# Start-up of a two-layer kernel on one core: first two token tiles enter the V projection centred, first V weights second in the load queue, dummy matmuls in the gaps

## The chip, the cores and the metric

The kernel runs on one core of one Trainium2 chip. The metric is the time of one execution in microseconds (us); lower is better. The kernel before was given with 1294.41 us, the median of 3 runs (1294.16 to 1294.68). Kernels of one group of runs were timed on one chip, interleaved with the kernel before; different groups fell on different chips.

A time is about 2.1 us longer than the span of the same run in the profile, which counts from the first to the last instruction. Times are compared with times and spans with spans.

## The reference

The model is a pair of blocks (local dilated attention, then a token-mixing MLP), run twice. Only the first lines of the first attention matter here:

```python
def _layernorm(x, axis=-1, eps=1e-5):
    m = jnp.mean(x, axis=axis, keepdims=True)
    v = jnp.var(x, axis=axis, keepdims=True)
    return (x - m) / jnp.sqrt(v + eps)
...
    # _A_ref: qkv = layernorm(x) @ wqkv, attention in a window of 8, dilation 2, then @ wo
    x = x + _A_ref(_layernorm(x, axis=-1), A_wqkv, A_wo)      # x: [1, 2048, 1024], wqkv: [1024, 3072]
    x = x + _B_ref(_layernorm(x, axis=-1), B_w1, B_b1, B_w2, B_b2)
    ...                                                        # both once more
```

## The kernel before

In lists and views, PE is TensorE, ACT is ScalarE, DVE is VectorE, and SP (SyncE) issues the loads; PSUM is the memory that TensorE writes its results to. All that the change touches is the function `start_up`, which loads the 16 token tiles (128 tokens x 1024 each), normalises them, transposes them to `hT` and multiplies them with the V weights. The first five tiles are transposed on TensorE (`tr`) and copied out of PSUM by ScalarE (`C_`), the others by DMA (`T_`). One tile passes: statistics on VectorE (`S_` twice, `A_`), 1/std on ScalarE (`R_`, a Ln and an Exp), normalisation on VectorE (`N_`), `tr`, `C_` in two halves, eight V matmuls per 512 output columns (`V_`), evacuation of PSUM on ScalarE (`E_`). Each engine gets its list in an order written by hand:

```python
    wm = m_tile()
    for _ in range(14):                    # dummy matmuls on zeros
        chain_("PE", lambda: nc.tensor.matmul(wm[:], lhsT=warm[:, 0:P], rhs=warm[:], start=True, stop=True))
    ...
    chain_("SP", x_load, 0, halves)        # load queue: tiles x0, x1, ... and halves of the V weights w(n, half)
    chain_("SP", x_load, 1)
    chain_("SP", w_load, 0, 0)
    chain_("SP", x_load, 2)
    chain_("SP", w_load, 0, 1)
    chain_("SP", x_load, 3)
    chain_("SP", w_load, 1, 0)
    chain_("SP", w_load, 1, 1)
    ...
    pe = [(tr, 0), (V_, 0, 0, lo4), (tr, 1), (V_, 0, 0, hi4), (V_, 1, 0, lo4), (tr, 2), (V_, 1, 0, hi4),
          (V_, 2, 0, a8), (V_, 0, 1, a8), (tr, 3), (V_, 1, 1, a8), (V_, 2, 1, a8), (tr, 4)]
    pe += [(V_, k, n, a8) for k in range(3, NT) for n in range(NDC)]
    act = [(R_, 0), (C_, 0, 0), (R_, 1), (C_, 0, 1), (C_, 1, 0), (C_, 1, 1), (R_, 2), (E_, 0, 0), (C_, 2, 0), (C_, 2, 1),
           (E_, 1, 0), (R_, 3), (E_, 2, 0), ...]
    dve = [(S_, 0, 0), (S_, 0, 1), (A_, 0), (S_, 1, 0), (N_, 0, halves), (S_, 1, 1), (A_, 1), (N_, 1, whole),
           (S_, 2, 0), (S_, 2, 1), (A_, 2)]
    ...
```

`(V_, k, n, lo4)` is the first half (four matmuls) of the V projection of tile k into columns 512n to 512n+511; it needs only the weight half w(n,0). V results share two PSUM buffers, so the third one waits for the evacuation of the first.

The softmax here doesn't subtract the row's maximum and nothing guards it: scores larger than these inputs give would overflow.

Of the kernel before, what the change touches and what calls it, by code (L numbers as in the profile page):

```python
# [9 lines left out]
ACT = mybir.ActivationFunctionType  # L10
# [15 lines left out]
def kernel(  # L26
# [58 lines left out]
    def m_tile():  # L85
        return psm.tile([P, 512], FP32, name="m", tag="m")
# [16 lines left out]
    def x2(name, shape=None, dt=BF16):  # L103
        return x2p.tile(shape or [P, D], dt, name=name, tag="x2")
# [4 lines left out]
    def st(name, shape):  # L109
        return stat.tile(shape, FP32, name=name, tag=name)  # L110

    def ln_exp_table():
        return tc.keep_in_program_order(nc.scalar.preload_act_table_set("natural_log_exp_and_others"))

    ln_exp_table()
    ident = const.tile([P, P], BF16, name="ident")
    make_identity(nc, ident[:])
    eps1 = const.tile([P, 1], FP32, name="eps1")
# [9 lines left out]
    for r in range(P // KG):  # L128
        hb_ = band[r * KG:(r + 1) * KG]
        nc.gpsimd.affine_select(out=hb_, in_=hb_, compare_op=ALU.is_ge, fill=0.0, base=0,  # L130
                                pattern=[[1, GW]], channel_multiplier=-1)
        nc.gpsimd.affine_select(out=hb_, in_=hb_, compare_op=ALU.is_ge, fill=0.0, base=W - 1,
                                pattern=[[-1, GW]], channel_multiplier=1)
    b1_bf = const.tile([P, FT], BF16, name="b1_bf")
    b2_bf = const.tile([P, NI, DIL], BF16, name="b2_bf")
    b1_sb = const.tile([P, FT], FP32, name="b1_sb")
# [35 lines left out]
    def rsqrt(dst, var, mul, eps):  # L172
        ln = st("ln", [P, 1])
        nc.scalar.activation(out=ln[:], in_=var, func=ACT.Ln, bias=eps[:], scale=mul)  # L174
        return nc.scalar.activation(out=dst, in_=ln[:], func=ACT.Exp, scale=-0.5)
# [9 lines left out]
        return mv[:, 0:1], rs  # L185

    def norm_dve(dst, x, mean, rs):
        return nc.vector.tensor_scalar(out=dst, in0=x, scalar1=mean, scalar2=rs[:], op0=ALU.subtract, op1=ALU.mult)

    def norm_act(dst, x, mean, rs):  # L190
        bi = st("bi", [P, 1])
# [8 lines left out]
    def chain_(eng, f, *args):  # L200
        with tc.issue_after(last[eng].ins) if eng in last else nullcontext():
            last[eng] = f(*args)

    def start_up(v, wv):
        np_ = 5
        warm = x2("warm", [P, 512])
        nc.vector.memset(warm[:], 0.0)
        xs, tps, pss_, mvs, sts, rss = {}, {}, {}, {}, {}, {}

        def x_load(k, hs=(slice(0, D),)):  # L210
            c, i = order[k]
            if k % 2 == 0:
                x_load.t = gop.tile([P, GF, D], BF16, name="x0", tag="go")
            xs[k] = x_load.t[:, k % 2, :]
            for h in hs:
                r = nc.sync.dma_start(out=xs[k][:, h], in_=xin_v[c, i][:, h])
            return r

        def w_load(n, hf):
            return nc.sync.dma_start(out=wv[n][hf][:], in_=wq_v[:, hf * (KD // 2):(hf + 1) * (KD // 2),  # L220
                                                                2 * D + n * 512:2 * D + (n + 1) * 512])

        def S_(k, cc):
            if cc == 0:
                sts[k] = st("bn", [P, NDC, 6])
            return nc.vector.bn_stats(out=sts[k][:, cc, :], in_=xs[k][:, cc * 512:(cc + 1) * 512])

        def A_(k):
            mvs[k] = st("mv", [P, 2])
            return nc.vector.bn_aggr(out=mvs[k][:], in_=sts[k][:])  # L230

        def R_(k):
            rss[k] = st("rs", [P, 1])
            return rsqrt(rss[k][:], mvs[k][:, 1:2], 1.0, eps1)

        def N_(k, hs):
            for h in hs:
                r = norm_dve(xs[k][:, h], xs[k][:, h], mvs[k][:, 0:1], rss[k])
            return r

        def tr(k):
            tps[k] = pss.tile([P, KD, P], BF16, name="s", tag="s")
            for kt in range(KD):
                r = nc.tensor.transpose(tps[k][:, kt, :], xs[k][:, kt * P:(kt + 1) * P], ident[:])
            return r

        def C_(k, hf):
            ks = slice(hf * KD // 2, (hf + 1) * KD // 2)
            return nc.scalar.copy(out=hT[:, ks, cols(*order[k])], in_=tps[k][:, ks, :])  # L249

        def V_(k, n, kts):
            if kts[0] == 0:
                pss_[k, n] = m_tile()
            for kt in kts:
                r = nc.tensor.matmul(pss_[k, n][:], lhsT=hT[:, kt, cols(*order[k])], rhs=wv[n][kt // 4][:, kt % 4, :],  # L255
                                     start=(kt == 0), stop=(kt == KD - 1))
            return r

        def E_(k, n):
            c, i = order[k]  # L260
            return nc.scalar.copy(out=v[c][i][:, n * 512:(n + 1) * 512], in_=pss_[k, n][:])

        def T_(k):
            return nc.sync.dma_start_transpose(out=hT[:, :, cols(*order[k])], in_=xs[k])

        wm = m_tile()
        for _ in range(14):
            chain_("PE", lambda: nc.tensor.matmul(wm[:], lhsT=warm[:, 0:P], rhs=warm[:], start=True, stop=True))  # L268

        halves = (slice(0, D // 2), slice(D // 2, D))  # L270
        whole = (slice(0, D),)
        chain_("SP", x_load, 0, halves)
        chain_("SP", x_load, 1)
        chain_("SP", w_load, 0, 0)
        chain_("SP", x_load, 2)
        chain_("SP", w_load, 0, 1)
        chain_("SP", x_load, 3)
        chain_("SP", w_load, 1, 0)
        chain_("SP", w_load, 1, 1)
        for k in range(4, NT):  # L280
            chain_("SP", x_load, k)

        lo4, hi4 = range(KD // 2), range(KD // 2, KD)
        a8 = range(KD)
        pe = [(tr, 0), (V_, 0, 0, lo4), (tr, 1), (V_, 0, 0, hi4), (V_, 1, 0, lo4), (tr, 2), (V_, 1, 0, hi4),
              (V_, 2, 0, a8), (V_, 0, 1, a8), (tr, 3), (V_, 1, 1, a8), (V_, 2, 1, a8), (tr, 4)]
        pe += [(V_, k, n, a8) for k in range(3, NT) for n in range(NDC)]
        act = [(R_, 0), (C_, 0, 0), (R_, 1), (C_, 0, 1), (C_, 1, 0), (C_, 1, 1), (R_, 2), (E_, 0, 0), (C_, 2, 0), (C_, 2, 1),
               (E_, 1, 0), (R_, 3), (E_, 2, 0), (R_, 4), (E_, 0, 1), (C_, 3, 0), (C_, 3, 1), (R_, 5), (E_, 1, 1), (R_, 6),
               (E_, 2, 1), (C_, 4, 0), (C_, 4, 1)]  # L290
        es = [(E_, k, n) for k in range(3, NT) for n in range(NDC)]
        rs = [(R_, k) for k in range(7, NT)]
        for j, e in enumerate(es):
            act.append(e)
            if rs and j % 4 != 3:
                act.append(rs.pop(0))
        dve = [(S_, 0, 0), (S_, 0, 1), (A_, 0), (S_, 1, 0), (N_, 0, halves), (S_, 1, 1), (A_, 1), (N_, 1, whole),
               (S_, 2, 0), (S_, 2, 1), (A_, 2)]
        for k in range(2, NT):
            nx = k + 1 < NT  # L300
            if nx:
                dve.append((S_, k + 1, 0))
            dve.append((N_, k, whole))
            if nx:
                dve += [(S_, k + 1, 1), (A_, k + 1)]
        dve.append((zero_fill,))
        dve.append((cast_biases,))
        sp = [(T_, k) for k in range(np_, NT)] + [(load_biases,)]
        qs = {"PE": pe, "ACT": act, "DVE": dve, "SP": sp}
        need = {cast_biases: lambda: (load_biases,) in done, R_: lambda k: k in mvs, N_: lambda k, h: k in rss, tr: lambda k: (N_, k) in done, C_: lambda k, hf: k in tps,  # L310
                V_: lambda k, n, kts: ((C_, k, 1 if kts[-1] == KD - 1 else 0) in done or (T_, k) in done), E_: lambda k, n: (V_, k, n) in done,
                T_: lambda k: (N_, k) in done}
        done = set()
        while any(qs.values()):
            for eng, q in qs.items():
                while q and (q[0][0] not in need or need[q[0][0]](*q[0][1:])):
                    f, *args = q.pop(0)
                    chain_(eng, f, *args)
                    if f is V_:
                        if args[2][-1] == KD - 1:  # L320
                            done.add((f, args[0], args[1]))
                    else:
                        done.add((f, *(args if f is C_ else args[:1])))

    def load_wv():
        return [[wt_("wv", [P, KD // 2, 512]) for _ in range(2)] for _ in range(NDC)]
# [256 lines left out]
    def gemm2(c, i, w2t, g, src, dst, to_hT):  # L583
# [17 lines left out]
            nc.sync.dma_start(out=dst, in_=xo[:])  # L601
        if to_hT:
            mean, rs = stats(xo, 1.0, eps1)
            norm_dve(xs[:], xo[:], mean, rs)
            nc.sync.dma_start_transpose(out=hT[:, :, cols(c, i)], in_=xs[:])

    NU = NG * DIL
# [124 lines left out]
```

## Time and profile before

| | before |
|---|---|
| time, median of 3 | 1294.41 us |
| span of the profiled run | 1293.7 us |
| TensorE (PE) busy | 1276.5 us, 99% |
| first V matmul | 8.61 us |
| V matmuls go on after the transposes of tile 4 | 21.54 us |

From the page, span and busy time of the engines:

```profile
span 1293.7 us, 19400 instructions
...
PE 1276.5 (99%) x8286; PEld 593.7 (46%) x8442; DVE 417.3 (32%) x852; ACT 373.2 (29%) x628; POOL 2.4 (0%) x15
```

TensorE is the limit, and the change can win only time in which it waits or does dummy work before the V stream is dense. This is TensorE's timeline at the start (start us, duration us, engine, line, what x count, in brackets the idle time just before it and what ended it):

```profile
1.38 6.11 PE L268 MATMUL m<-warm 128*128 128x512 bf16 x14 [1.38 <-DVE warm L207]
7.32 0.61 PE L244 MATMUL s<-ident,x 128*128 128x128 bf16 x8
8.61 1.04 PE L255 MATMUL m<-wv,hT 128*128 128x512 bf16 x4 [0.68 <-ACT hT L249]
9.62 0.62 PE L244 MATMUL s<-ident,x 128*128 128x128 bf16 x8
10.08 1.89 PE L255 MATMUL m<-wv,hT 128*128 128x512 bf16 x8
12.42 0.62 PE L244 MATMUL s<-ident,x 128*128 128x128 bf16 x8 [0.45 <-DVE x L188]
13.09 4.26 PE L255 MATMUL m<-wv,hT 128*128 128x512 bf16 x19
...
21.54 2.75 PE L255 MATMUL m<-wv,hT 128*128 128x512 bf16 x11
```

The dummies run to about 7.4 us, 0.427 us apart: the slow clock. Eight transposes of tile 0 follow, a wait for the copy to `hT`, the first four V matmuls, the transposes of tile 1, and so on; from 13.09 us on it is dense. The 0.2 us before 13.09 are no lost time: the record of one matmul is missing there. In the later look before_third, at the same code, this stretch has all 20 matmuls, from 0.46 us after the start of the transposes:

```profile
11.68 0.62 PE L244 MATMUL s<-ident,x 128*128 128x128 bf16 x8 [0.45 <-DVE x L188]
12.14 4.48 PE L255 MATMUL m<-wv,hT 128*128 128x512 bf16 x20
```

The last line of the timeline, 21.54, is a good measuring point: everything won or lost earlier stands in this instant. I call it the **stream instant**.

### The profile page before, as it was taken

The numbers are of one execution on the slowest core, as the hardware profiler recorded it, in microseconds if no ns is written. First come the engines' busy times: TensorE is split into PE (matmuls) and PEld (weight loads), VectorE is DVE, ScalarE is ACT, GpSimd is POOL, SyncE is SP. The second block draws the span as 40 slices with busy tenths as digits, with TensorE's granted clock in tenths as the row PEclk, the third lists the DMA queues.
The fourth block names the chain that finished last, engine by engine and source line by source line (L and its number), as shares of the span: only waits on it lengthen the run. The fifth ranks groups of instructions, "written<-read, shape, count | busy, mean of one in ns | idle before, by whom it ended". The sixth has DMA issues, their size and how long they took to land.

```text
span 1293.7 us, 19400 instructions
## 1 busy us (share of the span) xinstructions
PE 1276.5 (99%) x8286; PEld 593.7 (46%) x8442; DVE 417.3 (32%) x852; ACT 373.2 (29%) x628; POOL 2.4 (0%) x15
## 2 busy tenths in 40 slices
PE   9999999999999999999999999999999999999999
PEld 4444444444444444444444444444444444444444
DVE  7457767830000022322300667778100000111111
ACT  5456665541111100000023666644311111000000
POOL 0000000000000000000000000000000000000000
PEclk9999999999999999999999999999999999999999
DMA  7411123643222135456510111246422222334331
GB/s 236 82 44 48 51 80 122 204 138 90 65 78 80 57 101 148 124 155 147 130 33 1 46 51 49 80 151 209 125 66 86 78 59 78 105 106 135 118 92 33
DMA packets 201862, 125.54 MB, mean 97 GB/s; under 512 B 39984, under 2 KB 183600, under 8 KB 201776
## 3 DMA queue, kind: packets, MB, share of 16 engines
q1 hardware_dynamic: 201776, 124.30, 33.9%
q8 instruction: 66, 1.08, 0.3%
q14 instruction: 20, 0.16, 0.0%
HBM read 96.48 MB, written 16.78 MB: 88 GB/s over the span
## 4 chain that ended last, share of the span: by engine, by line
PE 98%; issue 1%; DVE 0%; DMA 0%; ACT 0%; SPq 0%
PE m L352 17%; PE s L594 15%; PE s L547 15%; PE m L467 8%; PE acc L547 7%; PE m L547 7%; PE acc L594 7%; PE m L594 7%; PE m L337 4%; PE m L255 4%; PE s L383 2%; PE acc L418 1%; PE acc L422 1%; PE m L268 0%; DMA qB<-qs 0%
## 5 line engine op out<-in xcount | busy, mean ns | idle before, releaser
L594 PEld LDWEIGHTS <-w 128*128 128x128 bf16 x1820 | 177.0, 98 | 210.2
L547 PEld LDWEIGHTS <-w 128*128 128x128 bf16 x1792 | 175.4, 98 | 211.4
L352 PE MATMUL m<-hT,wqk 128*128 128x512 bf16 x963 | 223.3, 379 | 6.2 <-issue 4.6
L547 PE MATMUL s<-h,w 128*128 128x512 bf16 x878 | 201.2, 379 | 0.8
L594 PE MATMUL s<-g,w 128*128 128x512 bf16 (+1 forms) x912 | 201.0, 374 | 0.7
L596 DVE SCALAR_TENSOR_TENSOR xo<-s,b_sb,xs 128x512 bf16<-128x512 f32 (+1 forms) x33 | 24.4, 739 | 532.9 <-PE s L594 527.6
L352 PEld LDWEIGHTS <-wqk 128*128 128x128 bf16 x1024 | 95.3, 98 | 117.9 <-issue 10.7
L398 DVE TENSOR_TENSOR Pm<-pc,band 32x640 bf16<-32x640 bf16 x256 | 123.5, 483 | 66.0 <-ACT pc L386 56.6
L467 PE MATMUL m<-wo,oT 128*128 128x512 bf16 x500 | 110.6, 379 | 0.8 <-issue 0.3
L547 PE MATMUL acc<-h,w 128*128 128x512 bf16 x440 | 103.1, 379 | 0.5
L594 PE MATMUL acc<-g,w 128*128 128x512 bf16 x436 | 99.7, 379 | 0.5
L547 PE MATMUL m<-h,w 128*128 128x512 bf16 x438 | 98.5, 379 | 0.5
L594 PE MATMUL m<-g,w 128*128 128x512 bf16 (+1 forms) x436 | 96.9, 376 | 0.6
L174 ACT ACTIVATE ln<-mv,eps 128x1 f32<-128x1 f32 x64 | 18.9, 295 | 221.1 <-DVE mv L182 184.9
L467 PEld LDWEIGHTS <-oT 128*128 128x128 bf16 x512 | 49.6, 98 | 60.3 <-issue 1.3
L554 ACT ACTIVATE g<-s,b_sb 128x1024 bf16<-128x1024 f32 x28 | 31.2, 1114 | 158.2 <-PE s L547 146.5
L363 DVE COPY qB<-qs 32x512 bf16<-32x512 bf16 x136 | 38.1, 280 | 90.5 <-ACT qs L359 89.2
L255 PE MATMUL m<-wv,hT 128*128 128x512 bf16 x250 | 55.6, 379 | 1.0 <-ACT hT L249 0.7
L337 PE MATMUL m<-wv,hT 128*128 128x512 bf16 x251 | 55.2, 379 | 0.3
L386 ACT ACTIVATE pc<-s,shift 128x640 bf16<-128x640 f32 x64 | 51.2, 800 | 12.2 <-PE s L383 12.1
L359 ACT CAST qs<-m 128x512 bf16<-128x512 f32 x64 | 37.5, 586 | 49.1 <-PE m L352 48.0
L356 ACT CAST kT<-m 128x512 bf16<-128x512 f32 x64 | 37.5, 586 | 46.4 <-PE m L352 46.4
(58 smaller groups left out, 675.1 us busy)
## 6 DMA issues: line engine op xcount, KB each, us to landing
w<-in_B_w_dram SPq DMA_DIRECT2D x56, 512.0 KB, 3.8
w<-in_B_w_dram SPq DMA_DIRECT2D x64, 448.0 KB, 4.5
wqk<-in_A_wqkv_dram SPq DMA_DIRECT2D x16, 512.0 KB, 4.8
xa<-xn SPq DMA_DIRECT2D x32, 256.0 KB, 2.2
xs<-xa SPq DMA_DIRECT2D x32, 256.0 KB, 3.1
wv<-in_A_wqkv_dram SPq DMA_DIRECT2D x8, 512.0 KB, 5.7
wo<-in_A_wo_dram SPq DMA_DIRECT2D x8, 512.0 KB, 6.0
xr<-in_A_x_dram SPq DMA_DIRECT2D x16, 256.0 KB, 3.3
```

The costliest lines, as they stand in the source:

```text
L255: r = nc.tensor.matmul(pss_[k, n][:], lhsT=hT[:, kt, cols(*order[k])], rhs=wv[n][kt // 4][:, kt % 4, :], start=(kt == 0), stop=(kt == KD - 1))
L337: nc.tensor.matmul(ps[:], lhsT=hT[:, kt, cols(c, i)], rhs=wv[n][kt // 4][:, kt % 4, :], start=(kt == 0), stop=(kt == KD - 1))
L352: mm = nc.tensor.matmul(ps[:], lhsT=wts[part][:, kt, (g % 2) * P:(g % 2 + 1) * P], rhs=hT[:, kt, lo:lo + 512], start=(kt == 0), stop=(kt = ...
L356: nc.scalar.copy(out=kT[u % 2][:, ls], in_=ps[:])
L359: nc.scalar.copy(out=qs[:], in_=ps[:])
L363: nc.vector.tensor_copy(out=qB[u % 2][hp, h, ls], in_=qs[hp, :])
L386: nc.scalar.activation(out=pc[:].rearrange("p (n t) h k -> p n (t h k)", n=2), in_=ss[:, :, 0:2 * HG * GW], func=ACT.Exp, scale=scale, bia ...
L398: mm = nc.vector.tensor_tensor(out=Pm[rp, :, s0:s0 + HB, r * KG:r * KG + GW].rearrange("p h t k -> p t h k"), in0=pc[rp], in1=mk, op=ALU.mult)
L467: mm = nc.tensor.matmul(ps[:], lhsT=oT[g][:, cols(c, i)], rhs=wo[n][g // 4][:, g % 4, :], start=(g == 0), stop=(g == NG - 1))
L547: nc.tensor.matmul(pairs[fl][0][dc], lhsT=wt[c][:, i, fl * P:(fl + 1) * P], rhs=h2[c][i][:, dc * 512:(dc + 1) * 512], start=(k == 0), stop ...
L554: nc.scalar.activation(out=g[fb][:, fl, :].rearrange("p (n d) -> p n d", n=2), in_=t[:], func=ACT.Gelu_apprx_tanh, bias=b1_sb[:, ft:ft + 1])
L594: nc.tensor.matmul(ap, lhsT=w2t[ft // HF][:, ft % HF, c::DIL], rhs=g[ft // GF][:, ft % GF, lo:lo + w], start=(ft == 0), stop=(ft == FT - 1))
```

## The change

Its intent: a LayerNorm can be split. Tiles 0 and 1 enter the matmul as x minus mean only, and 1/std multiplies the result in the evacuation, so Ln and Exp leave the path to the first matmul. Half of tile 0 is centred by ScalarE. The first V weights move ahead of x1 in the queue, to be there in time. There are ten dummies ahead instead of fourteen, and six dummies in gaps of TensorE (`(W_, n)` is n dummies), meant to keep its clock up. All dummies now write another PSUM buffer (`acc` in the views, before `m`). TensorE's order changes so that more V work stands ahead of the third tile. Since the Q and K projections need the normalised tiles 0 and 1, these are made later (`N_` after tiles 8 and 9, DMA transposes at the end of the list).

```diff
+        def M_(k, h):      # centre only
+            return nc.vector.tensor_scalar(out=xc[k][:, h], in0=xs[k][:, h], scalar1=mvs[k][:, 0:1], scalar2=None,
+                                           op0=ALU.subtract)
+        def Ma(k, h):      # the same on ScalarE, nm0 = -mean
+            return nc.scalar.activation(out=xc[k][:, h], in_=xs[k][:, h], func=ACT.Identity, bias=nm0[:])
...
-            return nc.scalar.copy(out=v[c][i][:, n * 512:(n + 1) * 512], in_=pss_[k, n][:])
+            dst, src = v[c][i][:, n * 512:(n + 1) * 512], pss_[k, n][:]
+            if k < 2:
+                return nc.scalar.activation(out=dst, in_=src, func=ACT.Identity, scale=rss[k])
+            return nc.scalar.copy(out=dst, in_=src)
...
-        for _ in range(14):
+        for _ in range(10):
...
         chain_("SP", x_load, 0, halves)
+        chain_("SP", w_load, 0, 0)
         chain_("SP", x_load, 1)
-        chain_("SP", w_load, 0, 0)
+        chain_("SP", w_load, 0, 1)
         chain_("SP", x_load, 2)
-        chain_("SP", w_load, 0, 1)
+        chain_("SP", w_load, 1, 0)
         chain_("SP", x_load, 3)
-        chain_("SP", w_load, 1, 0)
         chain_("SP", w_load, 1, 1)
...
-        pe = [(tr, 0), (V_, 0, 0, lo4), (tr, 1), (V_, 0, 0, hi4), (V_, 1, 0, lo4), (tr, 2), (V_, 1, 0, hi4),
-              (V_, 2, 0, a8), (V_, 0, 1, a8), (tr, 3), (V_, 1, 1, a8), (V_, 2, 1, a8), (tr, 4)]
+        pe = [(tr, 0), (W_, 2), (V_, 0, 0, lo4), (W_, 3), (tr, 1), (V_, 0, 0, hi4), (W_, 1), (V_, 1, 0, a8), (V_, 0, 1, lo4), (V_, 1, 1, lo4), (tr, 2),
+              (V_, 0, 1, hi4), (V_, 1, 1, hi4), (V_, 2, 0, a8), (tr, 3), (V_, 2, 1, a8), (tr, 4)]
-        act = [(R_, 0), (C_, 0, 0), (R_, 1), (C_, 0, 1), (C_, 1, 0), (C_, 1, 1), (R_, 2), (E_, 0, 0), (C_, 2, 0), (C_, 2, 1), ...
+        act = [(Ma, 0, halves[1]), (C_, 0, 0), (C_, 0, 1), (R_, 0), (C_, 1, 0), (C_, 1, 1), (R_, 1), (R_, 2), (E_, 0, 0),
+               (E_, 1, 0), (C_, 2, 0), (C_, 2, 1), (R_, 3), (E_, 0, 1), (E_, 1, 1), ...
...
-        sp = [(T_, k) for k in range(np_, NT)] + [(load_biases,)]
+        sp = [(T_, k) for k in (*range(np_, NT), 0, 1)] + [(load_biases,)]
```

More of the change, by code (lines that the diff above doesn't have):

```diff
@@ L113, in ln_exp_table @@
         return tc.keep_in_program_order(nc.scalar.preload_act_table_set("natural_log_exp_and_others"))
-    ln_exp_table()
     ident = const.tile([P, P], BF16, name="ident")
@@ L133 @@
                                 pattern=[[-1, GW]], channel_multiplier=1)
+    mv01 = const.tile([P, 2, 2], FP32, name="mv01")
+    rs01 = const.tile([P, 2], FP32, name="rs01")
+    nm0 = const.tile([P, 1], FP32, name="nm0")
     b1_bf = const.tile([P, FT], BF16, name="b1_bf")
@@ L187, in norm_dve @@
     def norm_dve(dst, x, mean, rs):
-        return nc.vector.tensor_scalar(out=dst, in0=x, scalar1=mean, scalar2=rs[:], op0=ALU.subtract, op1=ALU.mult)
+        return nc.vector.tensor_scalar(out=dst, in0=x, scalar1=mean, scalar2=rs, op0=ALU.subtract, op1=ALU.mult)
     def norm_act(dst, x, mean, rs):
@@ L205, in start_up @@
         np_ = 5
+        xc = [x2(f"xc{k}") for k in range(2)]
         warm = x2("warm", [P, 512])
@@ L228, in A_, with B_ @@
         def A_(k):
-            mvs[k] = st("mv", [P, 2])
-            return nc.vector.bn_aggr(out=mvs[k][:], in_=sts[k][:])
+            mvs[k] = mv01[:, k, :] if k < 2 else st("mv", [P, 2])[:]
+            return nc.vector.bn_aggr(out=mvs[k], in_=sts[k][:])
+        def B_(k):
+            return nc.vector.tensor_scalar(out=nm0[:], in0=mvs[k][:, 0:1], scalar1=-1.0, scalar2=None, op0=ALU.mult)
+        def M_(k, h):
[3 more added lines that the diff above has]
+            return nc.scalar.activation(out=xc[k][:, h], in_=xs[k][:, h], func=ACT.Identity, bias=nm0[:])
         def R_(k):
-            rss[k] = st("rs", [P, 1])
-            return rsqrt(rss[k][:], mvs[k][:, 1:2], 1.0, eps1)
+            rss[k] = rs01[:, k:k + 1] if k < 2 else st("rs", [P, 1])[:]
+            return rsqrt(rss[k], mvs[k][:, 1:2], 1.0, eps1)
         def N_(k, hs):
@@ L243, in tr @@
             for kt in range(KD):
-                r = nc.tensor.transpose(tps[k][:, kt, :], xs[k][:, kt * P:(kt + 1) * P], ident[:])
+                r = nc.tensor.transpose(tps[k][:, kt, :], (xc[k] if k < 2 else xs[k])[:, kt * P:(kt + 1) * P], ident[:])
             return r
@@ L260, in E_, with W_ @@
             c, i = order[k]
-            return nc.scalar.copy(out=v[c][i][:, n * 512:(n + 1) * 512], in_=pss_[k, n][:])
+            dst, src = v[c][i][:, n * 512:(n + 1) * 512], pss_[k, n][:]
+            if k < 2:
+                return nc.scalar.activation(out=dst, in_=src, func=ACT.Identity, scale=rss[k])
+            return nc.scalar.copy(out=dst, in_=src)
         def T_(k):
             return nc.sync.dma_start_transpose(out=hT[:, :, cols(*order[k])], in_=xs[k])
-        wm = m_tile()
-        for _ in range(14):
-            chain_("PE", lambda: nc.tensor.matmul(wm[:], lhsT=warm[:, 0:P], rhs=warm[:], start=True, stop=True))
+        wm = a_tile()
+        def W_(n):
+            for _ in range(n):
+                r = nc.tensor.matmul(wm[:, 0, :], lhsT=warm[:, 0:P], rhs=warm[:], start=True, stop=True)
+            return r
+        for _ in range(10):
+            chain_("PE", W_, 1)
         halves = (slice(0, D // 2), slice(D // 2, D))
         whole = (slice(0, D),)
+        chain_("ACT", ln_exp_table)
         chain_("SP", x_load, 0, halves)
+        chain_("SP", w_load, 0, 0)
         chain_("SP", x_load, 1)
-        chain_("SP", w_load, 0, 0)
+        chain_("SP", w_load, 0, 1)
         chain_("SP", x_load, 2)
-        chain_("SP", w_load, 0, 1)
+        chain_("SP", w_load, 1, 0)
         chain_("SP", x_load, 3)
-        chain_("SP", w_load, 1, 0)
         chain_("SP", w_load, 1, 1)
@@ L284, in start_up @@
         a8 = range(KD)
-        pe = [(tr, 0), (V_, 0, 0, lo4), (tr, 1), (V_, 0, 0, hi4), (V_, 1, 0, lo4), (tr, 2), (V_, 1, 0, hi4),
-              (V_, 2, 0, a8), (V_, 0, 1, a8), (tr, 3), (V_, 1, 1, a8), (V_, 2, 1, a8), (tr, 4)]
+        pe = [(tr, 0), (W_, 2), (V_, 0, 0, lo4), (W_, 3), (tr, 1), (V_, 0, 0, hi4), (W_, 1), (V_, 1, 0, a8), (V_, 0, 1, lo4), (V_, 1, 1, lo4), (tr, 2),
+              (V_, 0, 1, hi4), (V_, 1, 1, hi4), (V_, 2, 0, a8), (tr, 3), (V_, 2, 1, a8), (tr, 4)]
         pe += [(V_, k, n, a8) for k in range(3, NT) for n in range(NDC)]
-        act = [(R_, 0), (C_, 0, 0), (R_, 1), (C_, 0, 1), (C_, 1, 0), (C_, 1, 1), (R_, 2), (E_, 0, 0), (C_, 2, 0), (C_, 2, 1),
-               (E_, 1, 0), (R_, 3), (E_, 2, 0), (R_, 4), (E_, 0, 1), (C_, 3, 0), (C_, 3, 1), (R_, 5), (E_, 1, 1), (R_, 6),
-               (E_, 2, 1), (C_, 4, 0), (C_, 4, 1)]
+        act = [(Ma, 0, halves[1]), (C_, 0, 0), (C_, 0, 1), (R_, 0), (C_, 1, 0), (C_, 1, 1), (R_, 1), (R_, 2), (E_, 0, 0),
+               (E_, 1, 0), (C_, 2, 0), (C_, 2, 1), (R_, 3), (E_, 0, 1), (E_, 1, 1), (R_, 4), (C_, 3, 0), (C_, 3, 1), (E_, 2, 0),
+               (R_, 5), (C_, 4, 0), (C_, 4, 1), (E_, 2, 1), (R_, 6)]
         es = [(E_, k, n) for k in range(3, NT) for n in range(NDC)]
@@ L296, in start_up @@
                 act.append(rs.pop(0))
-        dve = [(S_, 0, 0), (S_, 0, 1), (A_, 0), (S_, 1, 0), (N_, 0, halves), (S_, 1, 1), (A_, 1), (N_, 1, whole),
+        dve = [(S_, 0, 0), (S_, 0, 1), (A_, 0), (B_, 0), (M_, 0, halves[0]), (S_, 1, 0), (S_, 1, 1), (A_, 1), (M_, 1, whole[0]),
                (S_, 2, 0), (S_, 2, 1), (A_, 2)]
@@ L305, in start_up @@
                 dve += [(S_, k + 1, 1), (A_, k + 1)]
+            if k in (8, 9):
+                dve.append((N_, k - 8, whole))
         dve.append((zero_fill,))
         dve.append((cast_biases,))
-        sp = [(T_, k) for k in range(np_, NT)] + [(load_biases,)]
+        sp = [(T_, k) for k in (*range(np_, NT), 0, 1)] + [(load_biases,)]
         qs = {"PE": pe, "ACT": act, "DVE": dve, "SP": sp}
-        need = {cast_biases: lambda: (load_biases,) in done, R_: lambda k: k in mvs, N_: lambda k, h: k in rss, tr: lambda k: (N_, k) in done, C_: lambda k, hf: k in tps,
-                V_: lambda k, n, kts: ((C_, k, 1 if kts[-1] == KD - 1 else 0) in done or (T_, k) in done), E_: lambda k, n: (V_, k, n) in done,
-                T_: lambda k: (N_, k) in done}
+        need = {cast_biases: lambda: (load_biases,) in done, R_: lambda k: k in mvs, N_: lambda k, h: k in rss, tr: lambda k: (N_, k) in done if k > 1 else (M_, k) in done and (k == 1 or (Ma, k) in done),
+                B_: lambda k: k in mvs, M_: lambda k, h: k in mvs, Ma: lambda k, h: (B_, k) in done, C_: lambda k, hf: k in tps,
+                V_: lambda k, n, kts: ((C_, k, 1 if kts[-1] == KD - 1 else 0) in done or (T_, k) in done), E_: lambda k, n: (V_, k, n) in done and k in rss,
+                T_: lambda k: (N_, k) in done and (k > 1 or (E_, k, 1) in done)}
         done = set()
@@ L322, in start_up @@
                     else:
-                        done.add((f, *(args if f is C_ else args[:1])))
+                        done.add((f, *(args if f in (C_, E_) else args[:1])))
     def load_wv():
@@ L603, in gemm2 @@
             mean, rs = stats(xo, 1.0, eps1)
-            norm_dve(xs[:], xo[:], mean, rs)
+            norm_dve(xs[:], xo[:], mean, rs[:])
             nc.sync.dma_start_transpose(out=hT[:, :, cols(c, i)], in_=xs[:])
```

## The prediction

> **What bounds the kernel.** TensorE. The page gives PE busy 1276.5 of 1293.7 us (99%), and the chain of waits is 98% PE. The change touches only the V projection of the first layer's start-up, so it can win only PE time lost before the V stream is dense, plus nothing or a loss later. In the chain of waits over the first 24 us the losses are: dummy matmuls until 7.49 us; tile 0's transposes to 7.95; the copy to hT (0.59 us) to 8.61, when the first V matmul starts; four V matmuls; the transposes of tile 1 at 9.65; then copy, Ln, Exp and normalisation (10.28 to 12.37) before the transposes of tile 2 at 12.42. From 13.09 us on PE is dense (V matmuls 0.216 to 0.219 us apart). After tr 4 the stream goes on at 21.70 us. Everything that can be won is a shift of that instant.
>
> **What the change moves.**
> - Tile 0: Ln and Exp (4.80 to 5.32) leave the path; a tiny DVE negation, a half-tile subtraction on DVE (0.40) and one on ACT replace them. Estimate for ACT: 0.59 us, the 128x512 copy[...]. Ready at about 5.65, not 6.1. Ten dummies end at about 5.7, not fourteen at 7.4 (0.427 us apart). So tr 0 at about 5.7, V at about 7.35, not 8.61.
> - Queue: the DMA landings of before are x1 4.7, w(0,0) 7.1, x2 7.8, w(0,1) 9.3, w(1,1) 13.0 us. Exchanged, I estimate w(0,0) at 6.2 and x1 at 7.0. So statistics of tile 1 (1.3 + 0.2) and its subtraction (0.55) end only at about 9.2: tr 1 at 9.2, not 9.65. Three dummies fill this gap.
> - Then V(1,0) whole and the first halves of V(0,1), V(1,1) go ahead of tr 2, which removes the 0.6 us idle at 12.4 and a 0.2 us restart.
> - Costs: one dummy on the path (0.22). V(2,0) needs the PSUM buffer of V(0,1), whose evacuation stands behind two copies and a Ln/Exp on ACT (about 2.0 us by the trace's spacing) while PE has only 1.75 us of matmuls: a new wait of about 0.3 to 0.55 us. [...]
> - Off the path: two normalisations and two DMA transposes (about 2.1 us each) behind the last one, ending near 48 us, and the wqk loads 4 us later, landing at about 57; QK starts at 66 us, so about 9 us of slack.
>
> **Sum.** tr 1 0.45 earlier, 0.8 of gap removed, 0.2 and 0.5 added: about 0.5 us gained, perhaps 1.5 if x1 lands early and the PSUM wait fails to appear. The rest of the kernel is shifted unchanged.
>
> **Clock.** The first dummies are spaced 0.427 us, V matmuls 0.216. The trace is at the fast rate by the transposes at 7.3. [...] Work plus dummies should keep PE busy from 1.4 to 8.9 us, so the fast rate should come near 7 us again. Failing that, each cold V matmul costs 0.21 us.
>
> **Prediction.** 1293.8 us, 8 in 10 between 1292.7 and 1294.6. Faster by over 2%: under 1%; within 2%: 99%; slower: under 1%.
>
> **Right or wrong.** Right if the first V matmul is at about 7.3 us, tr 1 waits for DVE (x1's statistics), no idle is left before tr 2, V(2,0) waits for ACT, and the V stream after tr 4 starts at about 21.2. Wrong if w(0,0) or x1 land over 0.5 us from my estimate, if V matmuls after 8 us are 0.43 us apart, or if QK's start waits for the late transposes or weights.

The sum is 0.45 + 0.8 - 0.2 - 0.5 = 0.55, "about 0.5 us". "Near 7 us again" is the author's estimate from one trace: TensorE was busy from 1.38 us on, and the matmuls from 7.32 us on ran fast.

## The result, and the profile after

The changed kernel took 1295.52 us (median of 6, 1295.26 to 1296.49); the kernel before in all its runs to then took 1295.06 us (median of 6, 1294.16 to 1295.55), of which the three taken beside the changed kernel were 1295.44, 1295.51 and 1295.55. The ratio is 1.0006, 95% interval 0.9993 to 1.0018. A ratio is the mean time of one kernel's runs over that of the other's, so it is not quite the ratio of the medians; this one takes all six runs of the kernel before. Against the three beside it alone, the means are 1295.68 and 1295.50 us, a ratio of 1.0001.

TensorE's timeline at the start of the changed kernel, columns as before:

```profile
1.38 4.45 PE L286 MATMUL acc<-warm 128*128 128x512 bf16 x10 [1.38 <-DVE warm L210]
5.62 0.98 PE L257 MATMUL s<-ident,xc 128*128 128x128 bf16 x8
6.44 0.59 PE L286 MATMUL acc<-warm 128*128 128x512 bf16 x2
7.28 1.04 PE L268 MATMUL m<-wv,hT 128*128 128x512 bf16 x4 [0.24 <-ACT hT L262]
8.15 0.81 PE L286 MATMUL acc<-warm 128*128 128x512 bf16 x3
9.08 0.62 PE L257 MATMUL s<-ident,xc 128*128 128x128 bf16 x8
9.54 1.03 PE L268 MATMUL m<-wv,hT 128*128 128x512 bf16 x4
10.40 0.38 PE L286 MATMUL acc<-warm 128*128 128x512 bf16 x1
10.62 3.69 PE L268 MATMUL m<-wv,hT 128*128 128x512 bf16 x15
14.14 0.61 PE L257 MATMUL s<-ident,x 128*128 128x128 bf16 x8
14.59 1.89 PE L268 MATMUL m<-wv,hT 128*128 128x512 bf16 x8
16.92 1.89 PE L268 MATMUL m<-wv,hT 128*128 128x512 bf16 x8 [0.44 <-ACT v L276]
...
21.26 5.00 PE L268 MATMUL m<-wv,hT 128*128 128x512 bf16 x21
```

The first V matmul comes 1.33 us earlier (7.28 against 8.61), the transposes of tile 1 only 0.54 (9.08 against 9.62), and the stream instant only 0.28 (21.26 against 21.54). VectorE's timeline shows why tile 1 gains less, and ScalarE's where the 0.44 us before 16.92 come from:

```profile
6.97 1.29 DVE L229 BATCH_NORM_STATS2 bn<-x 128x6 f32<-128x512 bf16 x2 [1.68 <-DMA x<-in_A_x_dram]
8.29 0.21 DVE L233 BATCH_NORM_AGGREGATE mv<-bn 128x2 f32<-128x12 f32 x1
8.54 0.48 DVE L239 TENSOR_SCALAR xc<-x,mv 128x1024 bf16<-128x1024 bf16 x1
```

```profile
14.79 1.07 ACT L262 COPY hT<-s 128x512 bf16<-128x512 bf16 x2 [1.56 <-PE s L257]
15.75 0.31 ACT L176 ACTIVATE ln<-mv,eps 128x1 f32<-128x1 f32 x1
16.09 0.20 ACT L177 ACTIVATE rs<-ln 128x1 f32<-128x1 f32 x1
16.20 1.25 ACT L276 ACTIVATE v<-m,rs 128x512 bf16<-128x512 f32 x2
```

x1 was 1.68 us late for VectorE (it landed at 4.7 us in the kernel before). And the first of the two evacuations that start at 16.20 us is the one that frees the PSUM buffer for tile 2's V matmuls; it stands behind two copies, a Ln and an Exp.

Both points, and the instants, were in the prediction. Yet the time did not fall. One loss was not in it, and it stands at the end of the program. The last VectorE instruction, in the kernel before (span 1293.7 us) and in the changed one (1293.4):

```profile
1291.05 0.35 DVE L596 SCALAR_TENSOR_TENSOR xo<-s,b_sb,xs 128x128 bf16<-128x128 f32 x1 [0.94 <-PE s L594]
1290.57 0.35 DVE L622 SCALAR_TENSOR_TENSOR xo<-s,b_sb,xs 128x128 bf16<-128x128 f32 x1 [0.95 <-PE s L620]
```

From its start to the end are 2.66 us before and 2.82 after; the whole stage, from the second MLP's first matmul to the end, takes 389.70 and 389.87 us, 0.17 more. In the traces, when the last output has landed, SyncE has one of its five closing waits left in the kernel before and four in the changed kernel. All nine looks at kernels with centring show this longer end, and none of the eight without. What orders these waits was not tried.

The start-up leaves the larger question, what the kernel before really does.

### The profile page after: what moved, and what is told of

Read it like the earlier page. It is cut to its first block, busy times and chain, and to the rows that moved or that the text cites. A ratio compares the mean times of both kernels' runs of the same rounds, so it can differ in the third digit from the quotient of the medians.

```text
span 1293.4 us, 19412 instructions
## 1 busy us (share of the span) xinstructions
PE 1276.5 (99%) x8288; PEld 594.0 (46%) x8444; DVE 417.9 (32%) x854; ACT 373.1 (29%) x629; POOL 2.4 (0%) x15
## 4 chain that ended last, share of the span: by engine, by line
PE 98%; issue 1%; DMA 1%; ACT 0%; DVE 0%; SPq 0%
PE m L378 17%; PE s L620 15%; PE s L573 15%; PE m L493 9%; PE acc L573 7%; PE m L573 7%; PE acc L620 7%; PE m L620 7%; PE m L363 4%; PE m L268 4%; PE s L409 2%; PE acc L444 1%; PE acc L448 1%; DMA x<-in_A_x_dram 0%; DMA qB<-qs 0%
```

## The experiments

The theories: A (the change is worth about 0.3 us, and the forecast's level was off because one kernel's time differs between sessions) against B (it costs up to 1 us in timed runs). After the first group came C (the kernel before is held by its fourteen dummies, whose end depends on the instant at which the clock is released: 7.49 us with a release at 7.31, 6.35 with one at 5.02), and then F against G (load order against centring).

"Release" below is the instant, from the start of the span, at which the trace's record of TensorE's granted clock begins. It agrees with the spacing of the dummies: 0.43 us before it and 0.22 us after it.

### Group 1: the kernel before against itself, the changed kernel again, and two parts of it undone

**before_again**: no edit.

> The kernel before, unchanged, timed against itself: the floor of the measurement. Theory A (the change is worth about 0.3 us, and the forecast missed because the same kernel reads up to 1 us differently from one session to another): ratio within 0.9995 to 1.0005, and the median of before may be up to 1 us from 1294.4. Theory B (the change really costs up to 1 us in the timed runs, by the instant at which the clock is released or by something later): the floor is the same, so this run tells nothing for or against B by itself, it only says what size can be seen at all. Both: clock record begins somewhere between 5 and 8.5 us from the start of the span, not always at 7.3[...].

Measured: 1294.96 us (median of 5, 1294.23 to 1295.41) against 1295.76 (9 runs), ratio 0.9994, interval 0.9981 to 1.0007. The same code differs from itself by 0.8 us, more than the 0.5 us of the forecast and more than theory A expected of this run; and 1295.76 is 1.35 us above the 1294.41 of the forecast, where A allowed 1 us. Its TensorE timeline:

```profile
1.38 4.97 PE L268 MATMUL m<-warm 128*128 128x512 bf16 x14 [1.38 <-DVE warm L207]
6.37 0.72 PE L244 MATMUL s<-ident,x 128*128 128x128 bf16 x8
7.76 1.04 PE L255 MATMUL m<-wv,hT 128*128 128x512 bf16 x4 [0.68 <-ACT hT L249]
...
20.69 3.62 PE L255 MATMUL m<-wv,hT 128*128 128x512 bf16 x15
```

The fourteen dummies took 4.97 us instead of 6.11, and all that follows is 0.85 us earlier, to the stream instant (20.69 against 21.54). The release was at 5.02 us here and at 7.31 in the trace that I had read: nearly all of that trace's dummies ran slow. In all looks told here but one the release falls anywhere from 4.04 us (x1_second) to 7.31; the one is told under combo_nocentre (10.21). What sets this instant was not shown.

**after_again**: no edit.

> The changed kernel, unchanged, in the same rounds. Theory A: 0.1 to 0.5 us faster than before of the same rounds, ratio 0.9996 to 1.0000; V stream after the transposes of tile 4 at 21.2 to 21.6 us in the trace. Theory B: 0.3 to 1 us slower, ratio 1.0002 to 1.0008, with the clock record beginning later than the first V matmul in the profile and V matmuls 0.43 us apart before it.

Measured: 1295.43 us (1295.23 to 1296.95), ratio 1.0000, interval 0.9988 to 1.0013. Release at 5.20 us, first V matmul at 6.90 instead of 7.28, but the stream instant 21.19 instead of 21.26. Here an early release hardly helps, because tile 1 waits for x1 (9.01 us). The time is at the edge of what A expected, and B's cold V matmuls are not there.

**x1_second**:

```diff
         chain_("SP", x_load, 0, halves)
-        chain_("SP", w_load, 0, 0)
         chain_("SP", x_load, 1)
+        chain_("SP", w_load, 0, 0)
         chain_("SP", w_load, 0, 1)
```

> The changed kernel with the old order of the first loads (x1 ahead of the first V weights). If the exchange in the queue is what holds tile 1 back: x1 lands at 4.7 instead of 6.95 us, its centring ends at about 7.4 instead of 9.03, and the transposes of tile 1 start when the three dummies end, at about 8.8 instead of 9.08; first V weights land at about 7.1, still ahead of the copy of tile 0 to hT, so the first V matmul stays at 7.3. Gain 0.25 us over the changed kernel at the V stream after the transposes of tile 4. If the exchange is needed (the intent of the change): the first V matmul moves to 7.8 or later and the stream is not earlier.

Measured: first V matmul at 7.11 us, transposes of tile 1 at 8.62, stream instant 20.81, 0.38 to 0.45 earlier than in the changed kernel's two traces (0.25 expected). 1294.88 us (1294.40 to 1295.68), ratio 0.9995, interval 0.9982 to 1.0007. The V weights came behind x1 at 7.1 us; in this run, with the earliest release (4.04), TensorE did wait 0.56 us for them, and it still gained. So, in this one look, moving the weights ahead of x1 costs more than it brings.

**e01_early**:

```diff
-               (E_, 1, 0), (C_, 2, 0), (C_, 2, 1), (R_, 3), (E_, 0, 1), (E_, 1, 1), ...
+               (E_, 1, 0), (C_, 2, 0), (E_, 0, 1), (C_, 2, 1), (R_, 3), (E_, 1, 1), ...
```

> The changed kernel with the evacuation of V(0,1) moved ahead of the second copy of tile 2 on ScalarE. If the 0.44 us idle of TensorE at 16.5 us is the PSUM buffer that waits behind two copies and a Ln/Exp on ScalarE: the wait falls under 0.1 us and the V stream after the transposes of tile 4 starts 0.4 us earlier (about 21.0), the whole span 0.4 us shorter. If the wait has another cause (weights w(1,1), which land at 12.3 to 13): it stays at 0.4 us.

Measured: the wait ahead of tile 2's V matmuls is gone, as TensorE's waits in the first 30 us show (what waited, for whom: us in total, times, longest):

```profile
PE acc L286 <- DVE warm L210: 1.4, 1, 1.4
PE m L268 <- ACT hT L262: 0.2, 1, 0.2
PE m L268 <- ACT v L276: 0.2, 1, 0.2
```

The wait of 0.2 us for `v` that remains is another one, at 12.66 us: the evacuation of V(0,0) stood behind the Ln and Exp of tile 2, whose load came at 9.9 us. So the stream instant was 20.98, 0.21 to 0.28 us earlier and not 0.4, and it was partly given back: Q and K start at 66.21 us, as in the changed kernel (66.24 and 66.17). 1295.27 us (1294.77 to 1296.45), ratio 0.9999, interval 0.9985 to 1.0013. The cause of the wait is confirmed, its worth is not.

### Group 2: the dummies, and a combination

**before_10**: the kernel before with

```diff
-        for _ in range(14):
+        for _ in range(10):
```

> The kernel before with 10 dummy matmuls instead of 14 and nothing else. Theory C: in the kernel before, what held tile 0 back in the trace of the forecast (first V matmul at 8.61 us) was not Ln and Exp but the fourteen dummies, which end at 7.49 us when the clock is released late (7.31) and at 6.36 when it is released early (5.02); with ten they end at 5.7 at the latest. Expected under C: first V matmul between 7.2 and 7.9 us whenever the clock is released, V stream after the transposes of tile 4 at 20.5 to 20.9 (before: 21.54 and 20.69 in its two traces; changed kernel: 21.26 and 21.19), so earlier than the changed kernel without any of its centring. In time: 0 to 0.8 us faster than before. Rival D (Ln, Exp and the normalisation are what holds tile 0, as the change assumes): first V matmul stays at 8.3 us or later.

Measured: C holds. First V matmul at 7.33 us with a rather late release (6.26), stream instant 20.36; the changed kernel had 21.26 with nearly the same release (6.39). That is 0.14 us earlier still than the range that C gave. 1295.18 us (five runs: 1293.48, 1293.74, 1295.18, 1295.18, 1296.63), ratio 0.9997, interval 0.9984 to 1.0009. TensorE's timeline:

```profile
1.38 4.45 PE L268 MATMUL m<-warm 128*128 128x512 bf16 x10 [1.38 <-DVE warm L207]
5.86 0.79 PE L244 MATMUL s<-ident,x 128*128 128x128 bf16 x8
7.33 1.04 PE L255 MATMUL m<-wv,hT 128*128 128x512 bf16 x4 [0.68 <-ACT hT L249]
8.34 0.62 PE L244 MATMUL s<-ident,x 128*128 128x128 bf16 x8
9.25 1.89 PE L255 MATMUL m<-wv,hT 128*128 128x512 bf16 x8 [0.29 <-DMA wv<-in_A_wqkv_dram]
```

One number changed, no centring, and the first V matmul is where the whole change puts it. The spread of the times is large; a possible cause is told under combo_nocentre.

**combo**: the changed kernel with

```diff
-        chain_("SP", w_load, 0, 0)
         chain_("SP", x_load, 1)
+        chain_("SP", w_load, 0, 0)
...
-        pe = [(tr, 0), (W_, 2), (V_, 0, 0, lo4), (W_, 3), (tr, 1), (V_, 0, 0, hi4), (W_, 1), (V_, 1, 0, a8), ...
+        pe = [(tr, 0), (W_, 2), (V_, 0, 0, lo4), (tr, 1), (V_, 0, 0, hi4), (V_, 1, 0, a8), ...
-        act = [..., (R_, 1), (R_, 2), (E_, 0, 0), (E_, 1, 0), (C_, 2, 0), (C_, 2, 1), (R_, 3), (E_, 0, 1), (E_, 1, 1), ...
+        act = [..., (R_, 1), (E_, 0, 0), (R_, 2), (E_, 1, 0), (C_, 2, 0), (E_, 0, 1), (C_, 2, 1), (R_, 3), (E_, 1, 1), ...
```

> The changed kernel with x1 second in the queue, no dummies after the first V half and none before V(1,0), the evacuation of V(0,0) ahead of the Ln/Exp of tile 2, and that of V(0,1) ahead of the second copy of tile 2. If the costs found in the changed kernel (tile 1 held by x1 and by three dummies, one dummy on the path, 0.44 us on the PSUM buffer of V(0,1)) add up: V stream after the transposes of tile 4 at 20.1 to 20.5 us, 0.7 to 1.1 earlier than the changed kernel, and the span that much shorter, except for the attention stages, which vary by up to 0.9 us between runs of one kernel. If the V weights of the first chunk (second half at about 8.7 us, third tile at 9.9) bound the start instead: 20.7 to 21.0.

Measured: 1293.85 us (1293.45 to 1294.96) against 1295.70 (9 runs, 1294.13 to 1295.93), ratio 0.9991, interval 0.9978 to 1.0003. Stream instant 19.71, better than expected:

```profile
7.17 1.04 PE L268 MATMUL m<-wv,hT 128*128 128x512 bf16 x4 [0.25 <-ACT hT L262]
8.05 0.61 PE L257 MATMUL s<-ident,xc 128*128 128x128 bf16 x8
8.73 4.55 PE L268 MATMUL m<-wv,hT 128*128 128x512 bf16 x20
13.12 0.61 PE L257 MATMUL s<-ident,x 128*128 128x128 bf16 x8
13.57 3.69 PE L268 MATMUL m<-wv,hT 128*128 128x512 bf16 x16
...
19.71 6.46 PE L268 MATMUL m<-wv,hT 128*128 128x512 bf16 x28
```

From 8.73 us on TensorE has no wait left in this stretch.

**no_gap_dummies**: the changed kernel without `(W_, 2)`, `(W_, 3)` and `(W_, 1)`.

> The changed kernel without the six dummies in the gaps. Theory C: the clock is released [...]at some instant between about 4 and 7.4 us[...]; so the dummies only cost, the one before V(1,0) 0.22 us, the three before tile 1 nothing, as tile 1 waits for x1. V stream after the transposes of tile 4 about 21.0. Rival E (the dummies hold the clock): V matmuls 0.43 us apart after 7.3 us, clock released later than 8 us, or throttled again, V stream 1 us or more later than the changed kernel's 21.2.

Measured: stream instant 21.34, not 21.0, so this size was missed: x1 came at 7.18 us in this run, tile 1's transposes started at 9.29 instead of 9.08, and that ate the 0.22 us of the missing dummy. The clock is what the run was for: release at 4.37 us, and after idle gaps of 0.68 us (before the first V matmul) and 1.41 us (7.9 to 9.3) the V matmuls still ran fast (four in 1.04 us and 20 in 4.63 us). Rival E does not hold in this look; a late release was not tested without the two dummies after `tr` of tile 0. 1295.00 us (1294.98 to 1295.48), ratio 0.9999, interval 0.9986 to 1.0013.

**before_third**: no edit, one look.

> A third look at the kernel before, for the instant at which the clock is released. Theory C: first V matmul between 7.5 and 8.65 us, the V stream after the transposes of tile 4 follows it at 12.93 us distance as in both earlier traces, and the later stages have the same lengths to 0.01 us except the two attention stages.

Measured: release at 5.82 us, first V matmul 7.87, stream instant 20.80, distance 12.93 us as expected. The stages after it have the same lengths in all four looks at the kernel before to 0.01 us, or differ by one missing matmul record (56.71 against 56.93 us), except the two attention stages, as expected.

### Group 3: is it centring or order?

**combo_again**: no edit to combo.

> The combination once more, to confirm it: V stream after the transposes of tile 4 at 19.6 to 20.0 us (19.71 in the first look); median 0.8 to 1.8 us under that of before of the same rounds (first time: 1293.85 against 1295.70).

Measured: stream instant 19.66, 1294.30 us (1293.68 to 1294.66) against 1295.80 (9 runs, 1294.85 to 1296.65), ratio 0.9989, interval 0.9977 to 1.0002. Every run of it is faster than every run of before in this group. The release was late (7.26) and the stream did not move, unlike that of the kernel before.

**combo_nocentre**: combo with tiles 0 and 1 normalised as in the kernel before:

```diff
-                r = nc.tensor.transpose(tps[k][:, kt, :], (xc[k] if k < 2 else xs[k])[:, kt * P:(kt + 1) * P], ident[:])
+                r = nc.tensor.transpose(tps[k][:, kt, :], xs[k][:, kt * P:(kt + 1) * P], ident[:])
-            if k < 2:
-                return nc.scalar.activation(out=dst, in_=src, func=ACT.Identity, scale=rss[k])
-        dve = [(S_, 0, 0), (S_, 0, 1), (A_, 0), (B_, 0), (M_, 0, halves[0]), (S_, 1, 0), (S_, 1, 1), (A_, 1), (M_, 1, whole[0]), ...
+        dve = [(S_, 0, 0), (S_, 0, 1), (A_, 0), (S_, 1, 0), (N_, 0, halves), (S_, 1, 1), (A_, 1), (N_, 1, whole), ...
...                                        # act starts as in the kernel before; no late N_ and T_ of tiles 0, 1
```

> The combination with its centring taken out: tiles 0 and 1 are normalised in place as in the kernel before, and the V evacuations are plain copies; queue, order of TensorE and dummies stay. Theory F (the gain of the combination comes from the order of the loads and of TensorE's work, and centring buys at most what stands between the normalised tile and the arrival of the first V weights at about 7.1 us): V stream after the transposes of tile 4 at 19.7 to 20.1, at most 0.3 us later than the combination. Theory G (centring is what brings the gain, as the change's intent says): 20.5 us or later.

Measured: 1294.11 us (1293.93 to 1295.77), ratio 0.9992, interval 0.9979 to 1.0004: by the median F, no slower than combo_again beside it. By the stream instant this look falls outside F (21.42 us, below), but for a reason that is not G's. The profiled run was the slowest of the five (1295.77), and its trace shows a late release:

```profile
1.38 4.45 PE L283 MATMUL acc<-warm 128*128 128x512 bf16 x10 [1.38 <-DVE warm L209]
6.66 1.03 PE L256 MATMUL s<-ident,x 128*128 128x128 bf16 x8 [0.83 <-DVE x L190]
7.49 1.06 PE L283 MATMUL acc<-warm 128*128 128x512 bf16 x2
8.37 1.89 PE L267 MATMUL m<-wv,hT 128*128 128x512 bf16 x4
```

x1 landed late here (its statistics start at 5.60 us), and the normalisation of tile 0 stands behind x1's first statistics in VectorE's list. TensorE was idle for 0.83 us, and the release came only at 10.21 us, against 4.04 to 7.31 in the other looks. That the idle time made it late was the author's estimate and was not shown. The first V matmuls ran at the slow clock (four in 1.89 us instead of 1.04), and the stream instant was 21.42, about 1.8 us later than in the second look below; 0.76 of this was there when the first transposes started (6.66 against 5.90).

**centre_only**: the changed kernel (ten dummies) with the queue, TensorE's order and ScalarE's order of the kernel before, and no dummies in gaps.

> Centring of tiles 0 and 1 and the 10 dummies, with the queue and TensorE's order of the kernel before and no dummies in gaps. Theory F: the first V matmul is at 7.1 us or a little later (bound by the first V weights), but the second half of V(0,0) waits for its weights, which land at about 9.2 us behind x2; V stream after the transposes of tile 4 at 20.2 to 20.5, no more than 0.15 us earlier than the kernel before with 10 dummies (20.36). Theory G: 19.9 or earlier.

Measured: first V matmul 7.37 us, stream instant 20.56, 0.06 outside what F expected, and no earlier than before_10 without centring (20.36, and 20.48 in a later look); G is out. 1294.31 us (1294.30 to 1295.08), ratio 0.9993, interval 0.9979 to 1.0007. TensorE's waits in the first 30 us name the limits: the copy, the third tile, the second weight half:

```profile
PE m L268 <- ACT hT L262: 0.7, 1, 0.7
PE s L257 <- DVE x L190: 0.5, 1, 0.5
PE m L268 <- DMA wv<-in_A_wqkv_dram: 0.2, 1, 0.2
```

**before_fourth**: no edit, one look.

> A fourth look at the kernel before, for the instant of the clock's release r. From its three looks (r 5.02, 5.82, 7.31 us: V stream after the transposes of tile 4 at 20.69, 20.80, 21.54): 20.65 to 20.72 if r is under 5.6, else 20.80 plus 0.5 times (r less 5.82), within 0.1 us.

Measured: stream instant 21.52. The trace has no record of the clock this time; all fourteen dummies ran 0.43 us apart (6.09 us in all) and the transposes at 7.31 us ran fast, so the release was near 7.3, for which the line through the earlier looks, in the expectation, gives 21.54. This run took 1296.98 us, though, because its attention stages were the longest seen (below).

### Group 4: three looks at what was open

**combo_nocentre_2**: no edit to combo_nocentre.

> Second look at the combination without centring. Theory F: with a release of the clock before 7.5 us, V stream after the transposes of tile 4 at 19.7 to 20.1 us. Theory G: 20.5 or later although the clock is released before 7.5. If the release is again later than 7.5 us[...], the look is void for F and G[...].

Measured: release 4.30, ahead of an idle gap of 0.76 us; stream instant 19.60, as good as with centring (19.71, 19.66). So the look says nothing of what a gap before the release does. F holds where the release is early. One run: 1294.32 us beside 1295.16 of before.

**before_10_2**: no edit to before_10.

> Second look at the kernel before with ten dummies. If the idle time between the tenth dummy (ends at about 5.8 us) and the first transposes is under 0.4 us: release before 7.5 us and V stream at 20.3 to 20.6. If it is 0.7 us or more and the release falls late: release near 10 us, V matmuls 0.43 us apart until then, V stream 21.4 or later.

Measured: idle of 0.32 us ahead of the first transposes, release 5.99, stream instant 20.48, 1294.05 us beside 1295.16. The late case of the expectation, which did not come up, is an estimate from the first look at combo_nocentre (idle 0.83 us, release 10.21, stream instant 21.42). Whether the slow timed runs of before_10 (1296.63) had late releases stays open, since no look at it fell on one. The record has a hint of something with the clock: the mean granted clock of the 1296.63 run and of one of the two of 1295.18 is 0.999, and that of every other run is 1.000. A share of 0.001 of a span of 1294 us is about 1.3 us (an estimate). But the look at the late release of combo_nocentre has 1.000, so the hint does not say what it was.

**after_third**: no edit to the changed kernel.

> Third look at the changed kernel: V stream after the transposes of tile 4 at 21.1 to 21.5 us whatever the release, since tile 1 waits for x1, which lands at about 7 us.

Measured: release 4.89, tile 1's transposes at 9.01, stream instant 21.18, 1295.33 us beside 1295.16.

### All looks at the two kernels together

| look | release, us | stream instant, us | Q and K start, us |
|---|---|---|---|
| before, the trace of the forecast | 7.31 | 21.54 | 66.43 |
| before_again | 5.02 | 20.69 | 65.58 |
| before_third | 5.82 | 20.80 | 65.69 |
| before_fourth | near 7.3 | 21.52 | 66.42 |
| changed kernel | 6.39 | 21.26 | 66.24 |
| after_again | 5.20 | 21.19 | 66.17 |
| after_third | 4.89 | 21.18 | 66.16 |
| combo, combo_again | 6.16, 7.26 | 19.71, 19.66 | 64.95, 64.89 |

`Q and K start` is the first matmul of the Q and K projections, after the last V matmul. Its mean is 66.03 us for the four looks at before and 66.19 for the three at the changed kernel. The change makes the start-up steadier, and on the mean of these few looks 0.16 us later.

## Why the prediction was right or wrong

It was wrong: 1295.52 us lies above the range (1292.7 to 1294.6), and no gain was measured where 0.5 us was forecast. The class (within 2%) was right, which says little: by the prediction's own first paragraph only a part of the first 24 us could be won.

- **TensorE as the limit, only the start-up matters**: right. Every stage outside the start-up and the two attention stages has the same length in both kernels, but for the 0.17 us at the end.
- **First V matmul at about 7.3, w(0,0) at 6.2, x1 at 7.0, tile 1 at 9.2**: right. Measured 7.28, 6.2 (issued at 1.72, landed 4.5 us later), 6.95 and 9.08.
- **New wait for ScalarE of 0.3 to 0.55 us before V(2,0)**: right, 0.44 us, and e01_early removes it.
- **Slack of the late transposes and loads**: right. The wqk loads are issued at 50.1 us instead of 48.3 (1.9 us later, not 4), and Q and K do not wait for them.
- **Clock**: right for the changed kernel. In its three looks the release is at 4.9 to 6.4 us, earlier than the 7 us forecast, and no V matmul runs slow. That busy time brings the release was not shown.
- **ScalarE's operands**: in the changed kernel the evacuation with a scale took 0.67 to 0.69 us, against 0.57 to 0.61 for the plain one. Tile 0's half, a 128x512 Identity with a bias that reads SBUF, took 0.72 us, against 0.59 on average for the copy out of PSUM in the kernel before.
- **The sum, "about 0.5 us gained"**: this is the step that failed. The waits and their order were as forecast; three terms of the sum were mis-sized.
  - "0.8 of gap removed": the "0.2 us restart" in it was the missing matmul record. Counted as the prediction counted, from start to start of the matmuls (the views' 0.45 and 0.44 us count from their modelled ends), 0.61 us was removed, and the new wait for ScalarE was 0.60 us where 0.5 was entered. From the transposes of tile 1 to the stream instant both kernels do 44 V matmuls; the changed one takes 12.18 us and the kernel before 11.92. So of the 0.54 us won at tile 1 only 0.28 is left at the stream instant.
  - "The rest of the kernel is shifted unchanged": it is not. The V stream from the stream instant to the start of Q and K lost 0.09 us (44.98 us instead of 44.89), and the end of the program 0.17. Against the very trace it was made from, about 0.02 us of gain is left (0.28 less 0.09 less 0.17). The rest of the 0.3 us between the two spans lies in the attention stages, which vary at the same code (next point).
  - "Ten dummies end at about 5.7 us, not fourteen at 7.4" took one late release for a property of the kernel. In before_again the fourteen took 4.97 us instead of 6.11, which puts the kernel before 0.85 us earlier, ahead of the changed kernel. Averaged over four looks there is no gain left to find.
- **The level**: "1293.8" was taken from a median of 1294.41 and a gain. The kernel before itself had 1295.44 to 1295.55 beside the changed kernel, 1295.76, 1295.70 and 1295.80 in the next three groups, and 1294.96 under another name. Its fast runs ranged from 1294.13 to 1296.65 us, all at a granted clock of 1.000, and the single look before_fourth, whose trace has no record of the clock, took 1296.98. The release moves its start by up to 0.85 us. The first attention stage (from the first scores to the first output projection) took 133.27 to 134.65 us and the second (from the second Q and K to its output projection) 140.26 to 141.22 over all looks told here, whose attention code is the same. That is another 1.4 and 1.0 us of range, which a range of 1.9 us around one session's median left no room for. What makes the attention stages vary was not tried and stays open.

The intent failed for a reason that the experiments show. Centring shortens a path that was held by other things: by the fourteen dummies in the kernel before (before_10), by x1 in the changed kernel (x1_second), by the copy in both (0.68 and 0.24 us), and by the V weights where x1 is loaded first (0.56 us in x1_second). With load order and TensorE's order put right the stream starts at 19.6 to 19.7 us with centring (two looks) or without (one look; the other one had a late release). What centring does bring is a smaller gap between ten dummies and the first transposes: up to 0.21 us of idle time (x1_second), against 0.03 (before_10) to 0.83 us (combo_nocentre) without it. In one look a late release, at 10.21 us, came with the gap of 0.83 us; that a smaller gap would have kept it early was not shown.

The combination beats both kernels in the traces: its stream starts 1.5 us ahead of the changed kernel and 1.0 to 1.9 ahead of the kernel before. Some of this is given back before Q and K (45.2 us from the stream instant to their start, against 44.9 and 45.0): these start 1.3 us ahead of the changed kernel's mean and 1.1 ahead of before's. The end of the program, 0.17 us longer with centring, takes a little more of its lead over before. In time its medians are 1.85 and 1.50 us under before in two groups. Both intervals just include 1, and the same code under two names differed by 0.8 us, so the times alone would be a thin proof.

## What to carry to other kernels

Before a start-up is tuned by fractions of a microsecond, look at several traces of the same code: here the instant of the clock's release, 5.02 to 7.31 us in the looks at the kernel before, made the start move by up to 0.85 us, and a plan built on one trace may win time that was never regularly lost. Taking work off a path pays only up to the next arrival. Here the loads' order, the order of TensorE's and ScalarE's lists and four dummies fewer moved the stream of the changed kernel by 1.5 us, and the arithmetic trick by next to nothing. And a sum of gains needs its losses to the end of the program: here about 0.26 us of 0.28 were lost again after the instant by which the start-up was judged. A dummy has to fill a gap that exists: the fourteen ahead, with a release at 7.31 us, put the first V matmul at 8.61, where ten, with one at 6.26, had it at 7.33. And look at the clock when time is lost behind them: in one look (combo_nocentre) the release came at 10.21 us, and four V matmuls took 1.89 us instead of 1.04.
